# The output projection of a decode kernel in two rows of each of two column groups, with one copy and two stores

## The chip, the cores and the metric

The kernel runs on one core of a Trainium2 chip. The metric is the device time of one execution in microseconds (us). The profile is of one execution; its span, from the first to the last instruction, is some 2.1 us shorter than the device time. Before the change the median was 1266.1 us of 3 runs (1266.0 to 1266.34).

## The reference

One token goes through grouped-query attention over a cache of 65,536 positions (16 query heads, 8 key/value heads of width 256), then through the output projection, and is mixed with a small MLP branch. Cut to what matters here:

```python
scores = jnp.einsum("bhqd,bhkd->bhqk", q, k) * (Dh ** -0.5)
p = _softmax(scores, axis=-1)
o = jnp.einsum("bhqk,bhkd->bhqd", p, v)
a = o.transpose(0, 2, 1, 3).reshape(B, Sq, Hq * Dh) @ wo      # 4096 -> 448
return g * a + (1 - g) * b                                    # b: the MLP branch, 448 values
```

The keys and values are 537 MB in bf16, and each byte is used once. The output is one row of 448 bf16 values, 896 bytes.

## The kernel before

Keys and values stream into SBUF in blocks of 8.39 MB. TensorE transposes the keys, VectorE and ScalarE copy the transposes out of PSUM, and TensorE makes scores and weighted sums. After each head pair TensorE multiplies its output by that pair's rows of `wo` and adds into the PSUM bank `prj`. The 448 output columns lie there as four pieces of 112, on partitions 0, 32, 64 and 96, one piece in each of four column groups. In the trace the matmuls of the four start within 10 ns (1261.488 to 1261.498 us), and the next one in a group 50 ns after the one before:

```python
NCG = 4
WG = DM // NCG                       # 112
def project(cols, i0=0):
    for i, j in enumerate(cols, i0):
        for q in range(NCG):
            ins = pe.matmul(prj[32 * q:32 * q + 1, 0:WG], oTn[:, j:j + 1],
                            wo_rows[:, i * DM + q * WG:i * DM + (q + 1) * WG], ...)
    return ins
```

The end of the program, for the last head pair (`sem_wl[h]` says that a half of its `wo` has landed):

```python
# TensorE
pe.wait_ge(s_oTn, H)
for h in range(REP):
    pe.wait_ge(sem_wl[h], 16)
    ins = project([dj * REP + h for dj in range(2)], 2 * h)     # 8 matmuls
ins.then_inc(s_proj, 1)
# VectorE (pieces 0 and 2); ScalarE does pieces 1 and 3 alike
vec.wait_ge(s_proj, H)
for q in range(0, NCG, 2):
    vec.tensor_copy(out_row[:, q * WG:(q + 1) * WG], prj[32 * q:32 * q + 1, 0:WG]).then_inc(s_fin, 1)
# SyncE
eng.wait_ge(s_fin, NCG)
eng.dma_start(out_ap, out_row[:, :]).then_inc(sem_out, 16)
eng.wait_ge(sem_out, 16)
```

The softmax here doesn't subtract the row's maximum and nothing guards it: scores larger than these inputs give would overflow.

Of the kernel before, what the change touches and what calls it, by code (L numbers as in the profile page):

```python
# [7 lines left out]
AF = mybir.ActivationFunctionType  # L8
# [4 lines left out]
def bass_gated_mix__gqa_block_cached__mixer_token_mlp__decode_kernel(  # L13
# [25 lines left out]
    P = 128  # L39
# [26 lines left out]
    pieces = [(NFIRST, NLATE), (NLATE, 124), (124, NV)]  # L66


    NCG = 4
    WG = DM // NCG  # L70
    assert WG * NCG == DM

    scale = 1.0 / (DH ** 0.5)
    GC0 = 0.796875
# [17 lines left out]
    with ctx:  # L92
# [49 lines left out]
        xc_row = scratch(1, DM, f32)  # L142
        scr_row = scratch(1, DM, f32)
        gu = sb([P, DM], bf16, "gu")
        w2cur = sb([P, 1], bf16, "w2cur")
        xcol = sb([P, WF + 2], bf16, "xcol")
        oTn = sb([P, 2 * REP], bf16, "oTn")
        accs = sb([P, SELC], f32, "accs")
        sel = sb([P, REP], f32, "sel")
        zrow = sb([1, NACC], bf16, "zrow")  # L150
# [9 lines left out]
        u_b = sb([P, DM], bf16, "u_b")  # L160
        z_b = sb([P, DM], bf16, "z_b")
        wtmp = sb([P, DM], bf16, "wtmp")
        out_row = sb([1, DM], bf16, "out_row")
        rest = sb([P, 1], bf16, "rest")
        bcast = sb([P, 3], f32, "bcast")
        brow1 = u_b[:, 0:WG]
        brow = z_b[:, 0:WG]
# [46 lines left out]
        block = ctx.enter_context(nc.Block())  # L214

        x_row_ap = A_x.rearrange("a b c -> (a b) c")
        out_ap = out.rearrange("a b n -> (a b) n")

        def src(cache, j, n0=0, n1=NV):
            g, m = divmod(j, PPH)  # L220
# [3 lines left out]
        @block.sync  # L224
        def _(eng):
            eng.dma_start(wq_a.rearrange("p j n -> p (j n)"),  # L226
                          A_wq[0:WF * P, :].rearrange("(p j) n -> p (j n)", p=P)).then_inc(sem_wq, 16)
            eng.dma_start(wq_b, A_wq[WF * P:DM, :].rearrange("r (a n) -> (r a) n", a=2)  # L228
                          ).then_inc(sem_wq, 16)
            def load(dst, cache, j, n0, n1, at, sem):  # L230
                eng.dma_start(dst[:, at + n0:at + n1, :].rearrange("p n d -> p (n d)"), src(cache, j, n0, n1)  # L231
                              ).then_inc(sem, 16)

            for j in range(NP):
                last = j == NP - 1
                if j >= 1:
                    eng.wait_ge(sem_tr[NB - 1], BODY * (j - 1) + DC)
                if j == 0:
                    load(kring, A_k_cache, j, HV, NV, 0, sem_k)
                    load(kring, A_k_cache, j, 0, HV, 0, sem_kb)  # L240
                elif last:
                    load(kring, A_k_cache, j, 0, HV, HV, sem_k)
                    load(kring, A_k_cache, j, HV, NV, HV, sem_kb)
                else:
                    load(kring, A_k_cache, j, 0, NV, HV * (j % 2), sem_k)
                if j == 0:
                    eng.wait_ge(s_q, 1)
                    eng.wait_ge(s_hb, 1)
                else:
                    eng.wait_ge(sem_pv, j)  # L250
                load(vbuf, A_v_cache, j, 0, NFIRST if last else NV, 0, sem_v)
                if last:
                    for (n0, n1), sem in zip(pieces, sem_vp):
                        load(vbuf, A_v_cache, j, n0, n1, 0, sem)
                g, m = divmod(j, PPH)
                if m == 0 and g < H - 1:
                    if g >= 1:
                        eng.wait_ge(s_proj, g)
                    w = A_wo[g * REP * DH:(g + 1) * REP * DH, :]
                    eng.dma_start(wo_rows, w.rearrange("(p i) n -> p (i n)", i=2 * REP)).then_inc(sem_wo, 16)  # L260

            eng.wait_ge(s_proj, H - 1)
            for h in range(REP):
                w = A_wo[(HQ - REP + h) * DH:(HQ - REP + h + 1) * DH, :]
                eng.dma_start(wo_sb[:, h, :], w.rearrange("(p j) n -> p (j n)", j=2)).then_inc(sem_wl[h], 16)  # L265
            eng.wait_ge(s_fin, NCG)
            eng.dma_start(out_ap, out_row[:, :]).then_inc(sem_out, 16)
            eng.wait_ge(sem_out, 16)

        @block.gpsimd  # L270
        def _(eng):
# [10 lines left out]
        def _(pe):  # L282
# [54 lines left out]
            def values(j, c0, u16):  # L337
                with pe.If(j == NP - 1):
                    pe.wait_ge(s_mix, 1)
                    for q in range(NCG):  # L340
                        r = slice(32 * q, 32 * q + 1)
                        pe.matmul(prj[r, 0:WG], rest[r, :], brow[r, :], start=False, stop=True,
                                  skip_group_check=True)
                    spin(8)
                pe.wait_ge(sem_exp, c0 + (BODY + 2))
                for r in range(BODY):
                    pe.matmul(acc[:, DENC:SELC], ones_sq[:, :], pT[:, r, :],  # L347
                              start=False, stop=(r == BODY - 1), skip_group_check=True)

                def some(n0, n1, last=False):  # L350
                    if last:
                        piece_wait(n0)
                    else:
                        pe.wait_ge(sem_v, u16)
                    for n in range(n0, n1):
                        r, nt = divmod(n, NT)
                        o = 32 * (n % 4)
                        ins = pe.matmul(acc[o:o + REP, 0:DH], pT[:, r, 2 * nt:2 * nt + 2], vbuf[:, n, :],  # L358
                                        start=False, stop=False, skip_group_check=True)
                    return ins  # L360

                some(0, NFIRST)
                with pe.If(j < NP - 1):
                    some(NFIRST, NV).then_inc(sem_pv, 1)
                with pe.Else():
                    some(NFIRST, NLATE, last=True).then_inc(s_early, 1)
                    tail()
# [33 lines left out]

            def project(cols, i0=0):
                for i, j in enumerate(cols, i0):
                    for q in range(NCG):
                        ins = pe.matmul(prj[32 * q:32 * q + 1, 0:WG], oTn[:, j:j + 1],  # L405
                                        wo_rows[:, i * DM + q * WG:i * DM + (q + 1) * WG],
                                        start=False, stop=True, skip_group_check=True)
                return ins


# [47 lines left out]
            with nc.Fori(0, H, 1, engines=on, head_slot={pe.engine: 0}) as g:  # L458
                with nc.Fori(0, PPH, 1, engines=on, head_slot={pe.engine: 0}) as m:
                    j = pe.snap(g * PPH + m, min_val=0, max_val=NP - 1)  # L460
                    c0 = pe.snap(j * BODY, min_val=0, max_val=NC)
                    u16 = pe.snap(j * 16 + 16, min_val=16, max_val=16 * NP)
                    keys(c0, j, u16, pe.snap(x2_reg, min_val=0, max_val=NV))
                    values(j, c0, u16)
                    with pe.If(j < FT):
                        pe.wait_ge(s_pb, j + 1)
                        for q in range(NCG):
                            pe.matmul(prj[32 * q:32 * q + 1, WG:2 * WG], w2cur[:, :],
                                      gu[:, q * WG:(q + 1) * WG], start=False, stop=True, skip_group_check=True)
                    pe.reg_sub(x2_reg, NV, x2_reg)  # L470
                with pe.If(g < H - 1):
                    pe.wait_ge(s_cp, g + 1)
# [7 lines left out]
        def _(vec):  # L480
            for b in range(0, NB, 2):
                vec.sem_inc(sem_ev[b], 1)
            vec.memset(xrem, 0.0)
            vec.memset(zrow[:, :], 0.0)
            vec.wait_ge(sem_ident, 1)
            vec.tensor_copy(identb, ident[0:3 * FT, 0:3 * FT]).then_inc(s_xrem, 1)
            vec.reduce_sum(sel[:, :], ident[:, :].rearrange("p (j n) -> p n j", j=4)[:, 0:REP, :], axis=AX.X)
# [50 lines left out]
            def mixer(j):  # L538
# [16 lines left out]
                vec.drain()  # L555
                vec.tensor_scalar(Z, Z, GC0, None, op0=ALU.mult).then_inc(s_u, 1)  # L556
                vec.tensor_scalar(W, U, 0.5, None, op0=ALU.mult)
                vec.tensor_copy(w2cur[:, :], w2p_b[:, bass.ds(kt, 1)])
                vec.wait_ge(s_tanh, j + 1)
                vec.tensor_scalar(Z, Z, 1.0, None, op0=ALU.add)  # L560
                vec.drain()
# [23 lines left out]
            def by_head(src):  # L585
                po_v = src.rearrange("p (dj hh) -> p dj hh", dj=2, hh=REP)
                r_v = rden[:, :].rearrange("p (o hh) -> p o hh", o=1).broadcast_to((P, 2, REP))
                vec.tensor_tensor(oTn[:, :].rearrange("p (dj hh) -> p dj hh", hh=REP), po_v, r_v,
                                  op=ALU.mult).then_inc(s_oTn, 1)

            def finish_head(g):
# [5 lines left out]
                    vec.tensor_copy(rrow[h, :], rden[h, hh:hh + 1])  # L597
                vec.drain()
                vec.wait_ge(s_sel, g + 1)
                vec.tensor_scalar(oTn[:, :], acc[:, SELC:NACC], rrow[:, :], None, op0=ALU.mult).then_inc(s_oTn, 1)  # L600

            vec.wait_ge(s_q, 1)
            vec.tensor_copy(qT[:, :, :].rearrange("p a b -> p (a b)"), sps[:, 1, 0:2 * HQ])
# [17 lines left out]
            vec.wait_ge(s_proj, H - 1)  # L621
            vec.tensor_copy(brow1, prj[:, WG:2 * WG])
            vec.drain()
            vec.tensor_copy(rest[:, :], bcast[:, 1:2])
            vec.tensor_scalar(brow, brow1, bcast[:, 2:3], None, op0=ALU.add).then_inc(s_mix, 1)
            with nc.Fori(NC - NCPH, NC, BODY, engines=on) as c0:
                for k in range(BODY):
# [2 lines left out]
            vec.wait_ge(s_late, 1)  # L630
            by_head(sps[:, 0, 0:2 * REP])
            vec.wait_ge(s_proj, H)
            for q in range(0, NCG, 2):
                vec.tensor_copy(out_row[:, q * WG:(q + 1) * WG], prj[32 * q:32 * q + 1, 0:WG]).then_inc(s_fin, 1)  # L634

        @block.scalar
        def _(act):
# [25 lines left out]
            with nc.Fori(0, NP, 1, engines=OrderedEngineSet([act.engine])) as j:  # L663
# [9 lines left out]
                with act.If(j < FT):  # L673
                    act.wait_ge(s_u, j + 1)
                    act.activation(z_b[:, :], z_b[:, :], AF.Tanh).then_inc(s_tanh, 1)  # L675
            act.wait_ge(s_proj, H)
            for q in range(1, NCG, 2):
                act.activation(out_row[:, q * WG:(q + 1) * WG], prj[32 * q:32 * q + 1, 0:WG], AF.Copy
                               ).then_inc(s_fin, 1)


# [26 lines left out]
```

## Time and profile before

| what | value | how to read it |
|---|---|---|
| device time | 1266.1 us | median of 3 |
| span | 1264.0 us | first to last instruction |
| data read | 544.22 MB at 431 GB/s | almost the whole span |
| TensorE busy | 73% | 31 waits for keys, 294.1 us in all (waits view) |
| last load landed | 1261.44 us | what comes later is the tail |
| tail | 2.57 us | 1264.01 - 1261.44; single records carry three decimals |

The lines are in the prediction. To read them, keep two regimes apart. Up to the last landing, as I read it, a later engine costs nothing as long as the DMA engines have a load queued: they are at nine tenths or more in 39 of 40 slices, and the big loads land 27.8 to 29.7 us after their issue. After it, every step on the way to the last instruction counts in full: these steps are the 2.57 us.

### The profile page before, as it was taken

Reading aid. Unit: us, or ns where it says so; the run is one execution under the profiler, and the core shown is the slowest. Engines: PE = TensorE matmul, PEld = TensorE weight load, DVE = VectorE, ACT = ScalarE, POOL = GpSimd, SP = SyncE. Lnnn points to the kernel's source line nnn. Section 1 sums busy time; section 2 is a strip of 40 time slices with the busy share of each in tenths; the row PEclk is TensorE's granted clock in tenths of the full one; section 3 lists DMA queues with packets and bytes.
Section 4 is the critical chain, followed back from the end, with each engine's and each line's share of the span. In section 5 each row is a group of like instructions: output and inputs, shape, how many; then the busy total and the mean of one; then the engine's idle time right before and its main releaser. Section 6 shows DMA issues by size and latency. Waiting matters only on the chain.

```text
span 1264.0 us, 38850 instructions
## 1 busy us (share of the span) xinstructions
PE 917.0 (73%) x17114; PEld 868.4 (69%) x17114; DVE 422.5 (33%) x764; ACT 538.2 (43%) x788; POOL 0.9 (0%) x7
## 2 busy tenths in 40 slices
PE   3876678766778667786676876758767688676688
PEld 2766668766677666786666876658766578666687
DVE  2433344333444333443222332323322233332233
ACT  1443345533355433454333553335533355433455
POOL 0000000000000000000000000000000000000000
PEclk9887788787898887987888987889887888877999
DMA  9999999999999999999999999999999999999998
GB/s 411 428 434 436 433 431 431 431 438 431 433 433 433 433 431 438 425 433 440 431 436 429 431 431 433 440 433 433 431 431 431 438 436 433 431 433 431 431 427 367
DMA packets 11623, 544.39 MB, mean 431 GB/s; under 512 B 1369, under 2 KB 1628, under 8 KB 2908
## 3 DMA queue, kind: packets, MB, share of 16 engines
q1 hardware_dynamic: 11522, 544.22, 99.7%
q8 instruction: 8, 0.13, 0.0%
q10 hardware_dynamic: 90, 0.01, 0.0%
q14 instruction: 3, 0.02, 0.0%
HBM read 544.22 MB, written 0.00 MB: 431 GB/s over the span
## 4 chain that ended last, share of the span: by engine, by line
DMA 70%; PE 29%; issue 1%; SPq 0%; DVEq 0%; DVE 0%; ACT 0%; ACTq 0%
DMA kring<-in_A_k_cache_dram 68%; PE kst L298 24%; PE sps L318 4%; DMA wo_sb<-in_A_wo_dram 2%; PE acc L358 0%; SPq L231 0%; SPq L265 0%; SPq L228 0%; SPq L226 0%; PE prj L405 0%; PE acc L347 0%; DVEq L92 0%; DVE out_row L634 0%; ACT pT L658 0%; ACTq L658 0%
## 5 line engine op out<-in xcount | busy, mean ns | idle before, releaser
L298 PE MATMUL kst<-ident,kring 128*128 128x128 f32 x4096 | 563.7, 299 | 304.9 <-DMA kring<-in_A_k_cache_dram 294.1
L669 ACT ACTIVATE ktT<-kst 128x1024 bf16<-128x1024 bf16 x512 | 500.0, 1021 | 667.3 <-PE kst L298 666.5
L298 PEld LDWEIGHTS kst<-ident,kring 128*128 128x128 f32 x4096 | 514.0, 156 | 314.8 <-issue 312.2
L569 DVE COPY ktT<-kst 128x1024 bf16<-128x1024 bf16 x512 | 354.2, 692 | 765.0 <-PE kst L298 742.0
L318 PEld LDWEIGHTS sps<-qcur,ktT 128*128 128x128 bf16 x8192 | 237.8, 96 | 4.1 <-issue 1.6
L318 PE MATMUL sps<-qcur,ktT 128*128 128x2 bf16 x8192 | 236.6, 163 | 1.3 <-issue 1.3
L358 PE MATMUL acc<-vbuf,pT 128*2 128x256 bf16 x4080 | 140.4, 305 | 3.8 <-issue 3.3
L358 PEld LDWEIGHTS acc<-vbuf,pT 128*2 128x2 bf16 x4080 | 105.2, 93 | 30.6 <-issue 3.8
L658 ACT ACTIVATE pT<-sps 128x32 f32 x256 | 51.8, 202 | 16.4 <-PE sps L318 16.4
L347 PE MATMUL acc<-pT,ones_sq 128*128 128x32 bf16 x256 | 11.7, 178 | 12.3 <-ACT pT L658 12.3
L347 PEld LDWEIGHTS acc<-pT,ones_sq 128*128 128x128 bf16 x256 | 8.6, 96 | 15.2 <-ACT pT L658 14.9
L675 ACT ACTIVATE z_b<-z_b 128x448 bf16<-128x448 bf16 x14 | 8.1, 577 | 20.5 <-DVE z_b L556 20.4
L575 DVE COPY accs<-acc 128x288 f32<-128x288 f32 x8 | 3.7, 458 | 38.5 <-PE acc L358 38.5
L394 PEld LDWEIGHTS acc<-sel,accs 128*64 128x64 f32 x112 | 10.8, 214 | 0.9
L394 PE MATMUL acc<-sel,accs 128*64 128x1 f32 x112 | 11.4, 260 | 0.0
L431 PE MATMUL acc<-vbuf 42*128 42x42 bf16 x1 | 0.2, 214 | 8.3 <-DMA b_b<-in_B_b_dram 8.3
L405 PE MATMUL prj<-wo_sb,oTn 128*1 128x112 bf16 x128 | 3.7, 244 | 3.1 <-DVE oTn L600 2.9
L431 PEld LDWEIGHTS acc<-vbuf 42*128 42x128 bf16 x1 | 0.1, 102 | 8.4 <-DMA b_b<-in_B_b_dram 8.4
L562 DVE TENSOR_TENSOR gu<-wtmp,z_b 128x448 bf16<-128x448 bf16 x14 | 5.5, 393 | 1.0
L554 DVE TENSOR_TENSOR z_b<-u_b,wtmp 128x448 bf16<-128x448 bf16 x14 | 5.5, 393 | 1.0
L550 DVE TENSOR_TENSOR z_b<-wtmp,u_b 128x448 bf16<-128x448 bf16 x14 | 5.5, 393 | 1.0
L548 DVE TENSOR_TENSOR wtmp<-u_b 128x448 bf16<-128x448 bf16 x14 | 5.5, 392 | 1.1
(89 smaller groups left out, 82.5 us busy)
## 6 DMA issues: line engine op xcount, KB each, us to landing
kring<-in_A_k_cache_dram SPq DMA_DIRECT2D x4, 4096.0 KB, 24.3
vbuf<-in_A_v_cache_dram SPq DMA_DIRECT2D x1, 6144.0 KB, 25.7
wo_sb<-in_A_wo_dram SPq DMA_DIRECT2D x7, 448.0 KB, 27.6
vbuf<-in_A_wq_dram SPq DMA_DIRECT2D x1, 3072.0 KB, 10.2
vbuf<-in_A_v_cache_dram SPq DMA_DIRECT2D x1, 1024.0 KB, 27.8
vbuf<-in_A_v_cache_dram SPq DMA_DIRECT2D x1, 768.0 KB, 28.9
vbuf<-in_A_wq_dram SPq DMA_DIRECT2D x1, 512.0 KB, 10.9
vbuf<-in_A_v_cache_dram SPq DMA_DIRECT2D x31, 29.7
```

Source lines behind the costliest of these rows:

```text
L298: ins = pe.transpose(kst[:, b, i * P:(i + 1) * P], kring_f[:, at + NT * (k % DC) + 4 * b + i, :], ident[:, :])
L318: ins = pe.matmul(sps[:, par, 2 * nt:2 * nt + 2], ktT[:, par, b, ntl * DH + dj:(ntl + 1) * DH:2], qcur[:, dj, :], start=(dj == 0), stop=(d ...
L347: pe.matmul(acc[:, DENC:SELC], ones_sq[:, :], pT[:, r, :], start=False, stop=(r == BODY - 1), skip_group_check=True)
L358: ins = pe.matmul(acc[o:o + REP, 0:DH], pT[:, r, 2 * nt:2 * nt + 2], vbuf[:, n, :], start=False, stop=False, skip_group_check=True)
L394: ins = pe.matmul(dst[hh * HP:(hh + 1) * HP, i:i + 1], accs[:, i:DH:2 * REP], sel[:, hh:hh + 1], start=False, stop=True, skip_group_check= ...
L548: vec.tensor_tensor(W, U, U, op=ALU.mult)
L550: vec.tensor_tensor(Z, W, U, op=ALU.mult)
L554: vec.tensor_tensor(Z, U, W, op=ALU.add)
L569: vec.tensor_copy(ktT[:, k % KTB, b, :], kst_b[:, b, :]).then_inc(sem_ev[b], 1)
L658: act.activation(pT[:, bass.ds(p0 + k % DC, 1), :].rearrange("p o n -> p (o n)"), sps[:, k % 2, 0:2 * NT], AF.Exp, scale=scale).then_inc(s ...
L669: act.activation(ktT[:, k % KTB, b, :], kst_b[:, b, :], AF.Copy).then_inc(sem_ev[b], 1)
L675: act.activation(z_b[:, :], z_b[:, :], AF.Tanh).then_inc(s_tanh, 1)
```

## The change

The intent is to shorten the tail. The projection's four pieces go to two rows in each of two column groups, so that one copy of 112 columns takes all of them out of PSUM and the two copies in a row on each engine become one. To put a piece on row 1 of a group, the weights become two columns wide, one of them zero, and the window slides over `oTw`. The rows then lie on partitions 0, 1, 32 and 33, and two engines store two rows each. Cut to its core:

```diff
-    NCG = 4
-    WG = DM // NCG
+    NCG = 2
+    NR = 2
+    WG = DM // (NCG * NR)
...
-        out_row = sb([1, DM], bf16, "out_row")
+        out_g = sb([P, WG], bf16, "out_g")
...
+        def store(eng, c):
+            eng.wait_ge(s_fin, 1)
+            eng.dma_start(out_ap[c * NR:(c + 1) * NR, :], out_g[group(c), :]).then_inc(sem_out, 16)
...
-                    for q in range(NCG):
-                        ins = pe.matmul(prj[32 * q:32 * q + 1, 0:WG], oTn[:, j:j + 1],
-                                        wo_rows[:, i * DM + q * WG:i * DM + (q + 1) * WG],
-                                        start=False, stop=True, skip_group_check=True)
+                    ins = spread(prj[:, 0:WG], oTw[:, j, :], wo_rows[:, i * DM:(i + 1) * DM])
+            def spread(dst, window, cols):
+                for r in range(NR):
+                    for c in range(NCG):
+                        q = c * NR + r
+                        ins = pe.matmul(dst[group(c), :], window[:, NR - 1 - r:2 * NR - 1 - r],
+                                        cols[:, q * WG:(q + 1) * WG], start=False, stop=True, skip_group_check=True)
...
-            for q in range(0, NCG, 2):
-                vec.tensor_copy(out_row[:, q * WG:(q + 1) * WG], prj[32 * q:32 * q + 1, 0:WG]).then_inc(s_fin, 1)
+            vec.tensor_copy(out_g[:, :], prj[:, 0:WG]).then_inc(s_fin, 1)
```

The mixer's projection and the bias follow the same layout, and ScalarE's copies give way to its store (cuts here).

More of the change, by code (lines that the diff above doesn't have):

```diff
@@ L66, in bass_gated_mix__gqa_block_cached__mixer_token_mlp__decode_kernel @@
     pieces = [(NFIRST, NLATE), (NLATE, 124), (124, NV)]
-    NCG = 4
-    WG = DM // NCG
-    assert WG * NCG == DM
+    NCG = 2
+    NR = 2
+    WG = DM // (NCG * NR)
+    assert WG * NCG * NR == DM
     scale = 1.0 / (DH ** 0.5)
@@ L144, in bass_gated_mix__gqa_block_cached__mixer_token_mlp__decode_kernel @@
         gu = sb([P, DM], bf16, "gu")
-        w2cur = sb([P, 1], bf16, "w2cur")
+        w2cur = sb([P, 2 * NR - 1], bf16, "w2cur")
         xcol = sb([P, WF + 2], bf16, "xcol")
-        oTn = sb([P, 2 * REP], bf16, "oTn")
+        oTw = sb([P, 2 * REP, 2 * NR - 1], bf16, "oTw")
+        oTn = oTw[:, :, NR - 1]
         accs = sb([P, SELC], f32, "accs")
@@ L162, in bass_gated_mix__gqa_block_cached__mixer_token_mlp__decode_kernel @@
         wtmp = sb([P, DM], bf16, "wtmp")
-        out_row = sb([1, DM], bf16, "out_row")
-        rest = sb([P, 1], bf16, "rest")
+        out_g = sb([P, WG], bf16, "out_g")
+        rest = sb([P, NR], bf16, "rest")
         bcast = sb([P, 3], f32, "bcast")
@@ L216, in bass_gated_mix__gqa_block_cached__mixer_token_mlp__decode_kernel, with group @@
         x_row_ap = A_x.rearrange("a b c -> (a b) c")
-        out_ap = out.rearrange("a b n -> (a b) n")
+        out_ap = out.rearrange("a b (q n) -> (a b q) n", q=NCG * NR)
+        def group(c):
+            return slice(32 * c, 32 * c + NR)
+        def store(eng, c):
+            eng.wait_ge(s_fin, 1)
+            eng.dma_start(out_ap[c * NR:(c + 1) * NR, :], out_g[group(c), :]).then_inc(sem_out, 16)
         def src(cache, j, n0=0, n1=NV):
@@ L265, in _ @@
                 eng.dma_start(wo_sb[:, h, :], w.rearrange("(p j) n -> p (j n)", j=2)).then_inc(sem_wl[h], 16)
-            eng.wait_ge(s_fin, NCG)
-            eng.dma_start(out_ap, out_row[:, :]).then_inc(sem_out, 16)
-            eng.wait_ge(sem_out, 16)
+            store(eng, 0)
+            eng.wait_ge(sem_out, 16 * NCG)
         @block.gpsimd
@@ L339, in values @@
                     pe.wait_ge(s_mix, 1)
-                    for q in range(NCG):
-                        r = slice(32 * q, 32 * q + 1)
-                        pe.matmul(prj[r, 0:WG], rest[r, :], brow[r, :], start=False, stop=True,
+                    for c in range(NCG):
+                        pe.matmul(prj[group(c), 0:WG], rest[group(c), :], brow[group(c), :], start=False, stop=True,
                                   skip_group_check=True)
@@ L403, in project @@
                 for i, j in enumerate(cols, i0):
-                    for q in range(NCG):
-                        ins = pe.matmul(prj[32 * q:32 * q + 1, 0:WG], oTn[:, j:j + 1],
-                                        wo_rows[:, i * DM + q * WG:i * DM + (q + 1) * WG],
-                                        start=False, stop=True, skip_group_check=True)
+                    ins = spread(prj[:, 0:WG], oTw[:, j, :], wo_rows[:, i * DM:(i + 1) * DM])
+                return ins
+            def spread(dst, window, cols):
+                for r in range(NR):
+                    for c in range(NCG):
+                        q = c * NR + r
+                        ins = pe.matmul(dst[group(c), :], window[:, NR - 1 - r:2 * NR - 1 - r],
+                                        cols[:, q * WG:(q + 1) * WG], start=False, stop=True, skip_group_check=True)
                 return ins
@@ L466, in _ @@
                         pe.wait_ge(s_pb, j + 1)
-                        for q in range(NCG):
-                            pe.matmul(prj[32 * q:32 * q + 1, WG:2 * WG], w2cur[:, :],
-                                      gu[:, q * WG:(q + 1) * WG], start=False, stop=True, skip_group_check=True)
+                        spread(prj[:, WG:2 * WG], w2cur[:, :], gu[:, :])
                     pe.reg_sub(x2_reg, NV, x2_reg)
@@ L484, in _ @@
             vec.memset(zrow[:, :], 0.0)
+            vec.memset(oTw[:, :, :], 0.0)
+            vec.memset(w2cur[:, :], 0.0)
             vec.wait_ge(sem_ident, 1)
@@ L557, in mixer @@
                 vec.tensor_scalar(W, U, 0.5, None, op0=ALU.mult)
-                vec.tensor_copy(w2cur[:, :], w2p_b[:, bass.ds(kt, 1)])
+                vec.tensor_copy(w2cur[:, NR - 1:NR], w2p_b[:, bass.ds(kt, 1)])
                 vec.wait_ge(s_tanh, j + 1)
@@ L587, in by_head @@
                 r_v = rden[:, :].rearrange("p (o hh) -> p o hh", o=1).broadcast_to((P, 2, REP))
-                vec.tensor_tensor(oTn[:, :].rearrange("p (dj hh) -> p dj hh", hh=REP), po_v, r_v,
+                vec.tensor_tensor(oTn.rearrange("p (dj hh) -> p dj hh", hh=REP), po_v, r_v,
                                   op=ALU.mult).then_inc(s_oTn, 1)
@@ L599, in finish_head @@
                 vec.wait_ge(s_sel, g + 1)
-                vec.tensor_scalar(oTn[:, :], acc[:, SELC:NACC], rrow[:, :], None, op0=ALU.mult).then_inc(s_oTn, 1)
+                vec.tensor_scalar(oTn, acc[:, SELC:NACC], rrow[:, :], None, op0=ALU.mult).then_inc(s_oTn, 1)
             vec.wait_ge(s_q, 1)
@@ L623, in _ @@
             vec.drain()
-            vec.tensor_copy(rest[:, :], bcast[:, 1:2])
+            for c in range(NCG):
+                vec.tensor_scalar(rest[group(c), :], ident[group(c), group(c)], bcast[group(c), 1:2], None,
+                                  op0=ALU.mult)
             vec.tensor_scalar(brow, brow1, bcast[:, 2:3], None, op0=ALU.add).then_inc(s_mix, 1)
@@ L675, in _ @@
                     act.activation(z_b[:, :], z_b[:, :], AF.Tanh).then_inc(s_tanh, 1)
-            act.wait_ge(s_proj, H)
-            for q in range(1, NCG, 2):
-                act.activation(out_row[:, q * WG:(q + 1) * WG], prj[32 * q:32 * q + 1, 0:WG], AF.Copy
-                               ).then_inc(s_fin, 1)
+            store(act, 1)
 _INS = ['A_x', 'A_k_cache', 'A_v_cache', 'A_wq', 'A_wo', 'B_x', 'B_w1', 'B_b1', 'B_w2', 'B_b2', 'gate_w']
```

## The prediction

> **What bounds the kernel now.** I read the page first, then the list of transfers, then the end of the chain of waits, then the timeline of the last microseconds, then the instructions on the tile `prj`. The page's slices and the shares of the chain show what kind of kernel it is:
>
> ```profile
> DMA  9999999999999999999999999999999999999998
> ...
> HBM read 544.22 MB, written 0.00 MB: 431 GB/s over the span
> ...
> DMA 70%; PE 29%; issue 1%; SPq 0%; DVEq 0%; DVE 0%; ACT 0%; ACTq 0%
> ```
>
> The 16 DMA engines are at nine tenths or more in 39 of 40 slices. TensorE's 29% of the chain is not time that TensorE costs: the chain follows the order of events (a tile lands, TensorE works on it, a buffer comes free, the next load is issued), and it doesn't show that the queue still holds another load meanwhile. The list of transfers does show it:
>
> ```profile
> vbuf<-in_A_v_cache_dram SPq DMA_DIRECT2D x31, 29.7
> kring<-in_A_k_cache_dram SPq DMA_DIRECT2D x30, 27.8
> ```
>
> One such load is 128 partitions of 128 x 256 bf16, 8.39 MB, which at 431 GB/s takes 19.5 us. From issue to landing it takes 27.8 us (keys) and 29.7 us (values). So a load is issued some 8 to 10 us before the engines get to it (27.8 - 19.5 and 29.7 - 19.5): that long can the compute side be late before the stream has a hole. The stream of 544 MB sets the time; what the compute engines do matters only after the last byte has landed. The chain's end shows when that is:
>
> ```profile
> 1232.11 29.33 DMA wo_sb<-in_A_wo_dram
> 1261.44 0.04 issue
> 1261.49 0.39 PE prj L405 x6
> 1261.87 0.02 issue
> 1261.90 0.26 DVE out_row L634
> 1262.16 0.30 DVEq L92
> ```
>
> The last load, the second half of the last two heads' `wo`, lands at 1261.44 us. From there to the end of the span, 1264.01 us, are 2.57 us that no stream covers. All that the change can gain or lose on the path lies in them. The timeline shows who does what there (columns: start, length, engine, line, what, count, idle time before):
>
> ```profile
> 1261.01 0.27 PE L405 MATMUL prj<-wo_sb,oTn 128*1 128x112 bf16 x8
> 1261.49 0.10 PEld L405 LDWEIGHTS prj<-wo_sb,oTn 128*1 128x1 bf16 x8 [0.38 <-DMA wo_sb<-in_A_wo_dram]
> 1261.49 0.35 PE L405 MATMUL prj<-wo_sb,oTn 128*1 128x112 bf16 x8 [0.21 <-DMA wo_sb<-in_A_wo_dram]
> 1261.90 0.54 ACT L678 ACTIVATE out_row<-prj 1x112 bf16<-1x112 f32 x2 [8.90 <-PE prj L405]
> 1261.90 0.56 DVE L634 CAST out_row<-prj 1x112 bf16<-1x112 f32 x2 [1.00 <-PE prj L405]
> 1262.49 0.32 SPq L267 DMA_DIRECT2D out_dram<-out_row  x1
> ```
>
> Five steps: wait for `wo` until 1261.44; eight matmuls, with the copies released at 1261.90; two copies each on VectorE and ScalarE side by side, the later pair done at 1262.46; the store issued on SyncE at 1262.49; its landing. The single records give the rest: the store's last semaphore update is at 1263.61, 1.13 us after the issue began, and SyncE goes on at 1263.63; the barrier at the program's end takes the remaining 0.38 us.
>
> [...] of the last eight matmuls the first four start at 1261.488, .492, .495 and .498 and the second four at 1261.538 to 1261.547. A column group takes its next matmul 50 ns after the one before. [...] 263 and 269 ns for the two of one partition and 274 ns for 128 partitions (below). [...] The store now is one packet of 896 bytes; the new one has rows of 224 bytes. No transfer of before writes such rows.
>
> **The change part by part.** The copies: the new copy takes all 128 partitions of 112 columns at once, and the kernel already has the same copy in the mixer's part, on the same bank:
>
> ```profile
> L622 DVE CAST u_b<-prj x1: 274/274/274, 1118.7 to 1118.7; 128x112 bf16<-128x112 f32 x1
> ```
>
> Today's copies run from 1261.897 to 1262.460, 0.563 us on VectorE; ScalarE's pair ends at 1262.435, beside it. One copy of 0.274 us in their place: -0.29 us. This is on the path.
>
> The matmuls: the number stays (four columns times four pieces of 112, 16 for a head pair, eight of them after the last landing). They go to two column groups, not four, with two weight columns, one of them zero. The width of the weights costs nothing that I can see: the value matmuls have two weight columns, stand in four groups, and go at 3.66 us for 128 in the timeline, 29 ns each, which is 256 columns by four groups. But eight matmuls in two groups are four rounds, not two. At 50 ns a round the last starts 150 ns after the first, not 50: +0.10 us on the path. The first eight, before the landing, also take 0.1 us more; they start at 1261.01 and have 0.21 us of idle time after them, so this stays hidden.
>
> The store: SyncE wakes 27 ns after the copy, as now. Two issues side by side rather than one, 0.32 us on SyncE; ScalarE's issues at the start of the kernel took 0.21 to 0.53 us. The end waits for the later of two landings, each of two packets of 224 bytes. I take the 1.13 us of today and +0.05 us for the later of two: a guess within the spread of those issue times.
>
> Elsewhere: the projections of seven heads (16 matmuls) and the mixer's four matmuls in each of 14 blocks have the same counts in half the groups. That is about 0.2 us more per head (four rounds more of 50 ns) and 0.05 us per block, against 8 to 10 us of loads waiting in the queue: hidden. The bias matmuls go from four to two, `rest` takes two small VectorE instructions rather than one, and two memsets come at the start. The first values' load is issued at 17.5 us, with 3.7 MB of `wq` and 8.4 MB of keys ahead of it (12.1 MB, 28 us at 431 GB/s): also hidden.
>
> The sum on the path: -0.29 + 0.10 + 0.05 = -0.14 us, so 1266.1 - 0.14 = 1265.96, put down as 1266.0 us.
>
> **The rivals.** (a) The small stores land late. If [...] the two queues' packets stand in each other's way, the landing could take 0.3 to 1 us more: 1266.3 to 1267.0 us. [...] Against it: of the 1.13 us only 0.04 us is the packet itself in the DMA records; the rest is issue, start and receipt[...]. (b) The two column groups eat all of the gain. If the matmuls of the two groups do not overlap, all eight follow one another at 50 ns, the last starts after 350 ns, not 50, and the path gets +0.30 rather than +0.10 us: 1266.2 us. Against it: the value matmuls and today's rounds overlap four deep. (c) The gain is larger: if the copies' release doesn't wait for the later rounds and the issue is shorter for two rows (0.21 us, the shortest of ScalarE's), the path gets -0.29 - 0.11 us: 1265.7 us. The release now comes 0.35 us after the last matmul's start, so it does seem to follow it. (d) The stream itself gets a hole through the later head ends, or goes at another rate: the same 544 MB, the same buffers and order speak against it. A hole would need 8 us of delay. A rate 0.1% off would be 1.3 us, more than all the rest, but the three runs of before lie within 0.34 us.
>
> **Range and chances.** The terms on the path are -0.29 (sure to 0.03), +0.10 (0 to +0.2), +0.05 (-0.1 to +0.5). The runs scatter by 0.34 us, more than the effect. I take 1265.6 to 1266.5 us for 8 in 10; above it stands rival (a) in its strong form. Two per cent is 25 us, ten times the whole uncovered tail, so within 2% has 0.98, and 0.01 is left on either side for something in the stream that I don't see.
>
> **What would show it.** In the changed profile's timeline from the last landing on: eight matmuls with the last start some 150 ns after the first (two rounds of 50 ns more); one VectorE copy of about 0.27 us with no ScalarE copy beside it; two issues, on SyncE and ScalarE, starting within 0.05 us of each other and 0.19 us earlier after the landing of `wo` than now; the store's last update about 1.1 to 1.2 us after them; DMA still 9 in 39 slices, and the landing of `wo` still near 1261.4 us. I am wrong on the store if issue to landing is over 1.3 us, on the groups if the copies' release comes more than 0.15 us later after the landing than today's 0.45 us, and on the whole if the last landing itself moves by over 0.5 us.

The three terms of the sum: -0.29 + 0.10 + 0.05 = -0.14 us. The first is the difference of two measured lengths (0.563 and 0.274 us), the second an estimate from the measured rounds of 50 ns, and the third a guess, as it says. Two measured numbers are missing there. The 29 ns for one value matmul are near an estimate from the trace of before: at clock 1.0 matmuls of 512 columns start 215 to 216 ns apart, so 256 columns in four groups at once would be 27 ns each. And the value matmuls do overlap four deep: four start within 10 to 11 ns, and the next four begin 98 to 99 ns later.

## The result, and the profile after

The changed kernel took 1266.24 us (median of 6, 1266.01 to 1266.42), the kernel before 1266.07 us (median of 6) in the same rounds. The ratio is 1.0001, with a 95% interval of 0.9988 to 1.0014. The time is the same, inside the predicted range, and the interval of about 1.7 us either way is far wider than the few tenths that the change is about. Only the traces can show those.

From the page of the changed kernel, the DMA engines' slices, what was read, and the chain's shares by engine:

```profile
DMA  9999999999999999999999999999999999999998
...
HBM read 544.22 MB, written 0.00 MB: 431 GB/s over the span
...
DMA 71%; PE 28%; issue 1%; SPq 0%; DVE 0%; ACT 0%; ACTq 0%
```

The stream is the same: 39 of 40 slices at nine tenths. From the list of transfers, the values' and keys' loads (count, median us from issue to landing):

```profile
vbuf<-in_A_v_cache_dram SPq DMA_DIRECT2D x31, 29.5
kring<-in_A_k_cache_dram SPq DMA_DIRECT2D x30, 27.9
```

29.5 and 27.9 us against 29.7 and 27.8: the loads wait in the queue as long as before. The end of the chain of waits (start, length, what):

```profile
1232.33 29.13 DMA wo_sb<-in_A_wo_dram
1261.46 0.04 issue
1261.51 0.38 PE prj L419 x8
1261.89 0.02 issue
1261.91 0.28 DVE out_g L648
```

The last load lands at 1261.46 us, within 0.02 us of before. The timeline of the tail:

```profile
1261.02 0.85 PE L419 MATMUL prj<-wo_sb,oTw 128*2 128x112 bf16 x16
1261.51 0.19 PEld L419 LDWEIGHTS prj<-wo_sb,oTw 128*2 128x2 bf16 x8 [0.30 <-DMA wo_sb<-in_A_wo_dram]
1261.91 0.28 DVE L648 CAST out_g<-prj 128x112 bf16<-128x112 f32 x1 [1.02 <-PE prj L419]
1262.22 0.33 SPq L227 DMA_DIRECT2D out_dram<-out_g  x1
1262.22 0.26 ACTq L227 DMA_DIRECT2D out_dram<-out_g  x1
```

One copy where there were two in a row, and two issues that start within 0.01 us of each other. The view of the instructions on `prj` has the length of the one copy, in ns (least, median, most):

```profile
L648 DVE CAST out_g<-prj x1: 275/275/275, 1261.9 to 1261.9; 128x112 bf16<-128x112 f32 x1
```

The single records split the tails of all runs. "Clock" is TensorE's granted clock (the share of full speed that the profile says was allowed) when the last eight matmuls start; "release" is from the first of those to the start of the copies; "store" is from the first issue's start to the last semaphore update of the stores. All in us:

| run | clock | landing to first matmul | release | copies | copy to issue | store | rest | tail |
|---|---|---|---|---|---|---|---|---|
| before, first trace | 0.5 | 0.044 | 0.409 | 0.563 | 0.027 | 1.126 | 0.397 | 2.566 |
| before again | 1.0 | 0.044 | 0.321 | 0.564 | 0.028 | 1.122 | 0.397 | 2.476 |
| changed, first trace | 1.0 | 0.044 | 0.404 | 0.275 | 0.028 | 1.275 | 0.397 | 2.423 |
| changed again | 1.0 | 0.045 | 0.403 | 0.275 | 0.027 | 1.280 | 0.397 | 2.427 |
| changed, stores swapped | 0.5 | 0.043 | 0.579 | 0.275 | 0.028 | 1.283 | 0.397 | 2.605 |
| changed, SyncE stores both | 0.5 | 0.045 | 0.578 | 0.275 | 0.027 | 1.464 | 0.397 | 2.786 |
| four groups, one copy | 1.0 | 0.044 | 0.322 | 0.274 | 0.028 | 1.654 | 0.393 | 2.715 |
| one group | 0.5 | 0.254 | 0.988 | 0.275 | 0.028 | 1.171 | 0.397 | 3.113 |
| before, two stores | 1.0 | 0.043 | 0.321 | 0.564 | 0.027 | 1.274 | 0.397 | 2.626 |

The first two traces alone tell a pleasant story: the tail went from 2.566 to 2.423 us, by -0.143, and the forecast sum was -0.14. But the terms don't fit it. The release did not get later (0.409 to 0.404) though it should have by 0.10, and the store took 0.15 us more, not 0.05. The experiments are about these two terms, and about whether later work elsewhere is hidden.

The stretches view explains the first. For the kernel before it shows TensorE's work on the projection just before the last landing and after it (stretch, its length, busy time and count of matmuls and of weight loads, granted clock, DMA share, GB/s):

```profile
1261.05:1261.30 0.25, 0.23 (x8) 0.06 (x8) 1.00 0.00 0
1261.49:1261.85 0.36, 0.35 (x8) 0.10 (x8) 0.50 0.00 0
```

For the changed kernel:

```profile
1261.05:1261.30 0.25, 0.25 (x8) 0.16 (x8) 1.00 0.00 0
1261.49:1261.85 0.36, 0.34 (x8) 0.19 (x8) 0.90 0.00 0
```

In the trace of before the clock fell to one half at 1261.30 us, just ahead of the last eight matmuls. In the trace of the changed kernel it fell at 1261.78 us, after they had all started. Their lengths agree: 250 to 298 ns before, 210 to 213 ns after. What sets the moment of the switch no run shows. In the traces every stretch at one clock is a multiple of 3.41 us long (the last is cut off by the end of the trace), and the switch falls anywhere from 1260.81 to 1264.21 us in the ten traces of programs with nearly the same tail, a spread of 3.40 us. The kernel before had its last eight matmuls at 0.5 in one trace and at 1.0 in the other. So I count their clock as chance: a pair of traces can differ by it.

### The profile page after: what moved, and what is told of

Same layout as the page of the kernel before. It is cut to its first block, busy times and chain, and to the rows that moved or that the text cites. A ratio compares the mean times of both kernels' runs of the same rounds, so it can differ in the third digit from the quotient of the medians.

```text
span 1263.9 us, 38847 instructions
## 1 busy us (share of the span) xinstructions
PE 924.7 (73%) x17112; PEld 870.7 (69%) x17112; DVE 422.6 (33%) x766; ACT 536.4 (42%) x786; POOL 0.9 (0%) x7
## 4 chain that ended last, share of the span: by engine, by line
DMA 71%; PE 28%; issue 1%; SPq 0%; DVE 0%; ACT 0%; ACTq 0%
DMA kring<-in_A_k_cache_dram 68%; PE kst L307 24%; PE sps L327 4%; DMA wo_sb<-in_A_wo_dram 2%; PE acc L366 0%; SPq L241 0%; SPq L275 0%; SPq L238 0%; SPq L236 0%; PE prj L419 0%; PE acc L355 0%; DVE out_g L648 0%; ACT pT L672 0%; ACTq L672 0%
## 5 line engine op out<-in xcount | busy, mean ns | idle before, releaser
L307 PE MATMUL kst<-ident,kring 128*128 128x128 f32 x4096 | 556.5, 297 | 297.0 <-DMA kring<-in_A_k_cache_dram 286.1
L307 PEld LDWEIGHTS kst<-ident,kring 128*128 128x128 f32 x4096 | 506.6, 154 | 306.4 <-issue 303.7
L366 PE MATMUL acc<-vbuf,pT 128*2 128x256 bf16 x4080 | 153.0, 322 | 5.4 <-issue 4.9
L366 PEld LDWEIGHTS acc<-vbuf,pT 128*2 128x2 bf16 x4080 | 112.0, 98 | 37.9 <-issue 5.2
L419 PE MATMUL prj<-wo_sb,oTw 128*2 128x112 bf16 x128 | 5.3, 232 | 3.1 <-DVE oTw L613 2.9
L419 PEld LDWEIGHTS prj<-wo_sb,oTw 128*2 128x2 bf16 x128 | 3.8, 90 | 4.0 <-issue 3.3
## 6 DMA issues: line engine op xcount, KB each, us to landing
vbuf<-in_A_wq_dram SPq DMA_DIRECT2D x1, 3072.0 KB, 10.3
vbuf<-in_A_v_cache_dram SPq DMA_DIRECT2D x31, 29.5
```

Of the source, the lines that this page charges most:

```text
L307: ins = pe.transpose(kst[:, b, i * P:(i + 1) * P], kring_f[:, at + NT * (k % DC) + 4 * b + i, :], ident[:, :])
L366: ins = pe.matmul(acc[o:o + REP, 0:DH], pT[:, r, 2 * nt:2 * nt + 2], vbuf[:, n, :], start=False, stop=False, skip_group_check=True)
L419: ins = pe.matmul(dst[group(c), :], window[:, NR - 1 - r:2 * NR - 1 - r], cols[:, q * WG:(q + 1) * WG], start=False, stop=True, skip_group ...
```

## The experiments

Each of the first four tests the release or the store; they ran on one chip. The theory was: rounds of matmuls in a group set the release, the clock explains the odd pair, and two stores that meet hinder each other. The rivals were a fixed floor under the release, and rows of 224 bytes that are slow by themselves.

**Four groups with one copy.**

```diff
-    NCG = 2
-    NR = 2
+    NCG = 4
+    NR = 1
...
-            eng.dma_start(out_ap[c * NR:(c + 1) * NR, :], out_g[group(c), :]).then_inc(sem_out, 16)   # on two engines
+            eng.dma_start(out_ap[:, :], out_g[0:128:32, :]).then_inc(sem_out, 16)                     # SyncE alone
```

> The change with four column groups of one row kept, one copy, and one store of four rows of 224 bytes by SyncE alone. Theory on the groups (rounds of 50 ns set the release; the clock was at half in the last batch before): the copy starts about 0.29 us after the first of the last eight matmuls if the granted clock there is 1.0, about 0.40 us if it is 0.5. Rival (a floor of 0.40 us that doesn't depend on the groups): 0.40 us at either clock. Theory on the store (the later of two transfers that meet on the same DMA engines lands late): one transfer lands 1.09 to 1.15 us after its issue begins. Rival (rows of 224 bytes are slow by themselves): 1.25 us or more. The time: 1265.8 us if both theories hold, within the scatter of the runs.

The release was 0.322 us at clock 1.0: no floor at 0.40, though my 0.29 was 0.03 too low. It is 0.08 us below the 0.404 of two groups at the same clock. The store was a surprise. Its line in the timeline:

```profile
1262.13 0.65 SPq L227 DMA_DIRECT2D out_dram<-out_g  x1
```

The issue alone takes 0.65 us and the store 1.654 us. So the tail is 2.715 us, the worst of the full-clock ones; the time was 1266.23 us (4 runs) against 1266.21 us (7 runs), ratio 1.0001, 0.9984 to 1.0017. By its letter the theory on the store (1.09 to 1.15 us) fails here and the rival (1.25 us or more) is met. But 1.654 us is far more than the 1.275 us that the rival was to explain, and the next run, with rows of the same size, shows that it is the rows' place that costs.

**One group of four rows.**

```diff
-    NCG = 2
-    NR = 2
+    NCG = 1
+    NR = 4
...
+            eng.dma_start(out_ap[:, :], out_g[0:4, :]).then_inc(sem_out, 16)                          # SyncE alone
```

> All four rows in one column group: eight rounds of the last eight matmuls, one copy, one store of four rows by SyncE. Theory on the groups: the last matmul starts 0.35 us after the first and the copy 0.58 to 0.60 us after the first at full clock (0.1 us for each doubling of rounds from two to four, 0.2 us from four to eight). Rival (the release is bound by something fixed): 0.40 us. Store: 1.09 to 1.15 us by the theory that two transfers hinder each other, 1.25 us or more by the rival that small rows are slow.

```profile
1263.00 0.35 SPq L227 DMA_DIRECT2D out_dram<-out_g  x1
```

That is the same four rows of 224 bytes, on partitions 0 to 3 rather than on every 32nd: issue 0.35 us, store 1.171 us. From the first packet's start to the last update both runs take 0.40 us; the difference lies ahead of it, as the first packet starts 1.254 us after the issue began there and 0.776 us here. Against 1.122 and 1.126 us for one row of 896 bytes, rows of 224 bytes cost at most 0.05 us by themselves. The release was 0.988 us at clock 0.5, with the last matmul 0.653 us after the first; TensorE was also still at the first half of the projection when the last load landed (0.254 us to the first matmul). The starts lie 93 to 94 ns apart, against 48 to 49 ns in the changed kernel at full clock, so the 0.58 to 0.60 us that I expected for full clock was not tested; but the floor is refuted again: more rounds, later release. The time: 1266.57 us.

**The stores swapped between the engines.**

```diff
-            store(eng, 0)
+            store(eng, 1)
...
-            store(act, 1)
+            store(act, 0)
```

> The changed kernel, but SyncE stores the rows of the second group and ScalarE those of the first. Theory (order decides: whichever transfer's packets start second waits for the other's): if ScalarE's packets again start first, SyncE's land last again, near 1.27 us after the issue, ScalarE's near 1.08 us. Rival (the rows or their addresses decide): the rows of the first group land late, now ScalarE's, near 1.27 us, and SyncE's near 1.1 us.

ScalarE's rows landed 1.095 us after its issue began, SyncE's 1.283 us, as in the changed kernel (1.086 and 1.275 us). So it is not the rows or their addresses. In both traces ScalarE's packets start first, by 0.02 to 0.03 us, and the last update follows 0.35 to 0.36 us after the first of them starts; for SyncE's it takes 0.51 to 0.52 us. Which update belongs to which store is inferred, as both count on one semaphore: I give the earlier updates to the packets that start earlier. The other way round, SyncE's would follow their packets by 0.31 to 0.32 us, less than the 0.34 us of a store that met no other (SyncE stores both, below). In every trace with two stores side by side SyncE's packets start second; no run turns that order round. This trace had the last matmuls at half clock (stretch, length, matmuls, weight loads, clock):

```profile
1261.63:1262.10 0.47, 0.47 (x10) 0.28 (x8) 0.50 0.00 0
```

Its release is 0.579 us, 0.17 us more than four groups at half clock (0.409). The time: 1266.39 us.

**The kernel before with its store cut in two.**

```diff
-            eng.dma_start(out_ap, out_row[:, :]).then_inc(sem_out, 16)
-            eng.wait_ge(sem_out, 16)
+            eng.dma_start(out_ap[:, 0:DM // 2], out_row[:, 0:DM // 2]).then_inc(sem_out, 16)
+            eng.wait_ge(sem_out, 32)
...
+            act.wait_ge(s_fin, NCG)
+            act.dma_start(out_ap[:, DM // 2:DM], out_row[:, DM // 2:DM]).then_inc(sem_out, 16)
```

> The kernel before, only its store cut in two halves of 448 bytes, one issued by SyncE and one by ScalarE. Theory (two transfers on the same DMA engine hinder each other): the later of them lands some 0.1 to 0.2 us later than the 1.13 us of the single store of 896 bytes. Rival (it was the 224 bytes or the two partitions): 1.13 us or less. The copies stay as before: 0.56 us. Copies' release 0.41 us after the first of the last matmuls at half clock, about 0.32 us at full clock.

```profile
1262.58 0.32 SPq L267 DMA_DIRECT2D out_dram<-out_row  x1
1262.59 0.24 ACTq L681 DMA_DIRECT2D out_dram<-out_row  x1
```

The store took 1.274 us, against 1.122 and 1.126 us for the same bytes in one transfer: +0.15 us from cutting it in two, with no other edit, one partition and rows of 448 bytes. That is as much as the whole surplus of the changed kernel, and the clean test of this term. The delay is not spread alike, though: here SyncE's packet starts 0.84 us after its issue began and its last update comes 0.43 us later; in the changed kernel it is 0.77 and 0.51 us, in the two traces of before 0.75 and 0.37 us. The time: 1266.2 us.

The second job ran on another chip.

**SyncE stores both.**

```diff
             store(eng, 0)
+            store(eng, 1)
...
-            store(act, 1)
```

> The changed kernel, but SyncE issues both stores, one after the other. By the issue times (0.33 us each on SyncE) the second begins about 0.36 us after the first, so it lands about 1.1 + 0.36 us after the first issue began if transfers that do not meet land in 1.1 us: 1.46 us. If the lateness comes from rows of 224 bytes or from SyncE's queue, 1.27 + 0.36 = 1.63 us.

```profile
1262.54 0.64 SPq L227 DMA_DIRECT2D out_dram<-out_g  x2
```

The stores begin 0.38 us apart. The first lands 1.109 us after its issue began, the second 1.084 us after its own: neither is late, and together they take 1.464 us. So SyncE's queue and rows of 224 bytes are not slow; two transfers that meet are. Two issuing engines save 1.464 - 1.275 = 0.19 us against one engine that issues both, only half of the 0.38 us by which the second issue moves up. Why meeting costs is not settled, and that the two share a DMA engine, as two of the expectations have it, is not shown: the packed records name a packet's queue and not its engine. The time: 1266.6 us.

**Later head ends.** The prediction called the doubled rounds at seven head ends hidden. I tried to make that lateness large:

```diff
                     pe.wait_ge(s_oTn, g + 1)
+                    spin(60)                      # 60 matmuls of 512 columns whose result nobody reads
                     project(range(2 * REP))
```

> The changed kernel with 60 idle matmuls of 512 columns (some 13 us at full clock) ahead of the projection at each of the seven head ends, to test that lateness there is hidden. Reading of the prediction taken by its letter (8 to 10 us of loads wait in the queue, and that is all the slack): the stream gets a hole of 3 to 5 us seven times, 21 to 35 us more. Fuller theory (TensorE also idles 6 to 7 us after each head end until the next keys land, so slack is about 6.5 + 8.4 = 15 us): no change, 1266 us within 0.5 us. Rival (head ends are on the path): 90 us more.

The 13 us for 60 matmuls is an estimate: such matmuls start 215 to 216 ns apart at clock 1.0 in the trace of before. It took 1399.37 us, 133 us more, which none of the three had expected. From its page, the DMA slices and the instruction queue (packets, MB, share of the 16 engines):

```profile
DMA  9999995999959999699996999959999699995998
...
q8 instruction: 72, 1.18, 0.3%
```

and from its timeline after the first head end (last bracket: idle time before, and what ended it):

```profile
196.33 0.56 PE L419 MATMUL prj<-wo_sb,oTw 128*2 128x112 bf16 x16
210.07 6.33 PE L307 MATMUL kst<-ident,kring 128*128 128x128 f32 x32 [13.18 <-issue]
```

The keys for that block had landed at about 188 us, and yet TensorE sat for 13.18 us, and not for data ("issue"). The instruction queue moved 72 pieces of 16,384 bytes; in the changed kernel it moved 8, all before 72 us:

```profile
q8 instruction: 8, 0.13, 0.0%
```

Nine pieces move in each of the seven later passes of the loop over heads. I read that as TensorE fetching its program again in every such pass. The single records tie the wait to it: at each of the seven head ends TensorE goes on 1.72 to 1.86 us after a piece has moved, the second of those that start during the wait. The lateness that I wanted to test is not told apart from that.

**The same with 120.** Only the count differs, `spin(120)`.

> The same with 120 idle matmuls, some 26 us. Fuller theory: 26 - 15 = 11 us of hole seven times, 70 to 80 us more (about 1340 us), and slices in which the DMA share falls below nine tenths. Prediction by its letter: 16 to 18 us seven times, 110 to 125 us more. On the path throughout: 180 us more.

It took 1429.97 us with 72 instruction pieces again: 30.6 us more than with 60, some 4 us for each head end, though the 60 further matmuls take 11.6 us there: the wait is only 6.3 us after the first head end, where only 0.5 MB of loads move meanwhile (DMA records). The figure I expected, 1340 us, failed for the same reason as before.

**Lateness in a loop.**

```diff
                     pe.wait_ge(s_oTn, g + 1)
+                    with nc.Fori(0, 12, 1, engines=on, head_slot={pe.engine: 0}):
+                        spin(4)
                     project(range(2 * REP))
```

> The changed kernel with 48 idle matmuls ahead of the projection at each of seven head ends, as 12 passes of a loop of four, so that the program grows by four matmuls only: 10 to 14 us of lateness without a larger program. Theory (TensorE idles 6 to 7 us after a head end and 8.4 us of loads wait in the queue, some 15 us of slack; the 133 us of the straight-line version came from 16384-byte pieces of program fetched behind the stream): 1266 us within 0.6 us, 8 transfers on the instruction queue. Rival (lateness itself costs, nothing to do with program size): 100 us or more, as in the straight-line version.

1394.23 us, and again 72 pieces. From its timeline:

```profile
207.89 6.29 PE L307 MATMUL kst<-ident,kring 128*128 128x128 f32 x32 [13.85 <-issue]
```

This run failed as a test. The cause may be my own `head_slot`, but no run without it tests that. It still shows one of the two parts of the slack. The keys of the next block are issued at 219.38 us, and in the changed kernel at 200.05 us. The stretches of this run (length, then matmuls, weight loads, VectorE, ScalarE, GpSimd, clock, DMA share, GB/s) show when the engines ran dry:

```profile
200.00:205.00 5.00, 0.00 (x0) 0.00 (x0) 0.00 (x0) 0.00 (x0) 0.00 (x0) 0.50 1.03 446
205.00:210.00 5.00, 2.11 (x10) 2.12 (x11) 0.69 (x1) 0.05 (x1) 0.00 (x0) 0.50 0.45 176
210.00:215.00 5.00, 5.00 (x58) 4.99 (x57) 2.08 (x3) 3.63 (x4) 0.00 (x0) 0.68 0.00 1
```

From 200 us on, when the next load is usually issued, the first two stretches moved 5 x 446 + 5 x 176 kB, or 3.1 MB: 7.2 us of stream at 431 GB/s. It faded rather than stopped, and its last packet starts at 210.2 us (DMA records). So the queue's cushion is 7 to 10 us, near the 8 to 10 us of the prediction.

**The loop with 24 passes.** Only the count differs.

> The same with 24 passes, 20 to 28 us of lateness at each head end. Theory of 15 us of slack: 5 to 13 us of hole seven times, 35 to 90 us more, 8 transfers on the instruction queue. If the only slack were the 8 to 10 us of the queue: 80 to 130 us more. If it is hidden altogether: 0.

1427.22 us, 72 pieces. The same fault; no reading of the slack follows. But the wait at the head end is shorter than with 12 passes, as in the run with 120 matmuls:

```profile
213.59 6.19 PE L307 MATMUL kst<-ident,kring 128*128 128x128 f32 x32 [9.81 <-issue]
```

In all four costly runs, at all 28 head ends, TensorE goes on 1.70 to 1.87 us after the second piece of program that starts in the wait has moved. So I take this wait to be for program. It takes 12.7 to 15.4 us in the two runs in which 3.7 to 6.3 MB of loads move meanwhile, and 6.3 to 10.3 us in the two with at most 1.6 MB, which fits pieces that move behind the loads.

**The 60 matmuls in a branch that is never taken.**

```diff
+                    with pe.If(g == H):
+                        spin(60)
```

> The changed kernel with the 60 idle matmuls in a branch that is never taken: their code lies in TensorE's program and none runs. Theory (the larger program is what costs): well over 2% slower and far more than 8 transfers on the instruction queue. Rival (the time of the matmuls costs): 1266 us within 0.6 us, 8 transfers.

1266.2 us, 9 pieces, and from its page:

```profile
DMA  9999999999999999999999999999999999999998
...
q8 instruction: 9, 0.15, 0.0%
```

So the larger program cost nothing here beyond one piece more and the scatter (1266.2 us against 1266.0 us, one look each): this expectation of mine fell. What the costly runs share is that longer code was run inside the loop. Why pieces then move in every pass was not shown; I did not vary the length in steps. Whether 13 us of pure lateness would be hidden stays open, and so the "hidden" of the prediction rests on the time and the slices of the changed kernel, not on these runs.

**Both kernels once more.** They were run at other times.

> The changed kernel once more, for the scatter. Theory (the effect on the tail is -0.1 to -0.2 us[...]): from the last load's landing to the end 2.42 us at full clock in the last batch, about 0.13 us more at half clock; the landing itself moves by some tenths of a us from trace to trace. Rival (the trace's tail was a lucky one and the change really costs 0.1 us): a tail of 2.57 us or more.

> The kernel before once more, for the tail. Theory (the release of the copies depends on the granted clock in the last batch): at clock 1.0 the copies start 0.32 us after the first of the last eight matmuls and the tail from the last landing to the end is 2.48 us; at clock 0.5, 0.41 us and 2.57 us. Against the changed kernel's 2.43 us at clock 1.0, the change is then worth 0.05 us on the path. Rival (the trace of before was typical whatever the clock): 0.41 us and 2.57 us at clock 1.0 too.

Before again, the stretch of the last eight matmuls:

```profile
1261.67:1261.90 0.23, 0.23 (x8) 0.10 (x8) 1.00 0.00 0
```

At clock 1.0 the release was 0.321 us and the tail 2.476 us, as expected; the rival (0.41 and 2.57 us whatever the clock) is refuted. The changed kernel repeated its tail to 0.004 us (2.427 us). Its time was 1266.2 us (4 runs) against 1266.0 us (7 runs), ratio 1.0002, 0.9985 to 1.0019. The last landing was at 1261.63 us in this trace of before and at 1261.51 us in that of the changed kernel: it moves by 0.1 to 0.2 us from trace to trace, as much as the change is about.

No version came out that beats both. The best terms measured are the release of four groups (0.32), the one copy (0.275) and the single store from one partition (1.12), but the copy leaves the rows on several partitions, and the stores from there cost 1.17 to 1.65 us or need more rounds.

## Why the prediction was right, and where not

The range and the class were right, and for the reason given: the stream sets the time, and the change acts on a tail of 2.5 us. The sum, -0.14 us, was not right, though the first pair of traces shows just that number. At equal clock the change is worth 2.425 - 2.476 = -0.05 us at clock 1.0 (mean of the two traces) and 2.605 - 2.566 = +0.04 us at clock 0.5 (the swapped run, whose stores differ only in which engine has which rows). So it is worth nothing that can be told from zero in the time. By the prediction's own terms:

- **The copies, -0.29:** right. 0.563 us became 0.275 us, -0.288.
- **The groups, +0.10:** right in mechanism, and in size at full clock, +0.083 (0.404 - 0.321). At half clock it is +0.170 (0.579 - 0.409): the third and fourth rounds then start 91 to 94 ns after the round before, not 50. What failed is the reading beneath it: the prediction took the release of before, 0.35 us after the last matmul's start, as typical; at clock 1.0 it is 0.26 us, in both kernels. The granted clock of that stretch stood in the profile, and it was 0.5. The bound that the prediction set itself, 0.15 us later than today's 0.45 us, is kept in both traces of the changed kernel, at clock 1.0, and passed by the swapped run at half clock (0.62 us), so that keeping it was partly luck. The issues came 0.29 us earlier after the landing in the first pair of traces, and 0.21 us at equal clock 1.0; 0.19 us was predicted.
- **The store, +0.05:** a mis-sized term. It is +0.15, shown by cutting the store of before in two. The guess was taken from the spread of the issue times, and not from what two transfers do to each other. The failure bound that the prediction set itself, 1.3 us from issue to landing, was just kept.
- **Rival (a):** right in direction. Rows of 224 bytes cost at most 0.05 us and two queues that meet 0.15 us, less than its 0.3 to 1 us, a guess with no measurement behind it. So is part of the ground against it, that the steps around the packet don't grow with rows: four neighbouring rows took 0.35 us to issue, but four on every 32nd partition 0.65 us. And the trace of before was not without small packets: 42 of 256 bytes came in at the start (DMA records).
- **Rival (b):** wrong. The two groups overlap: pairs start 3 to 4 ns apart, rounds 48 to 49 ns. Two weight columns cost no more than 1 ns a round there: rounds were 48 ns apart with one column, at clock 1.0 in the trace of before.
- **Rival (c):** did not come true. At equal clock the release does follow the later rounds, and SyncE's issue of two rows takes 0.33 us, not 0.21.
- **Elsewhere hidden, and rival (d):** the loads wait as long as before, no slice lost its nine tenths, and the time is the same. The forced test did not isolate it, as TensorE waited in it for what I take to be program (6.3 to 15.4 us at each head end of the four costly runs).

Where the expected gain went: -0.288 from the copies was given back as +0.083 (or +0.170) in TensorE's rounds and +0.15 in the meeting stores. Whether some tenth of the time's +0.17 us is real cannot be told from runs that scatter by 0.4 us.

## What to carry to other kernels

In a kernel bound by a stream, find the last landing and split what follows into its single terms; then compare term by term, and read the granted clock of each short stretch before two traces are compared, since a sum can agree by chance. A layout that saves a copy may have to pay for how its result is then produced and stored, here +0.083 and +0.15 us for -0.288 us. Before adding code to a loop in order to test lateness, look at the instruction queue of the result (72 pieces against 8 here), or the test may measure the waits that came with those pieces.
